# Seven products of quarters for the up product of three groups and the down product of all nine, a bank for the zeros, and a new order

## The chip, the cores and the metric

The kernel runs on one core of a Trainium2 chip. Its time is the time of one execution on the device, in microseconds (us). TensorE multiplies matrices into PSUM, an accumulator memory of eight banks of 2 KB a partition; VectorE (DVE) and ScalarE (ACT) read PSUM and the main on-chip memory, SBUF; GpSimd (POOL) works on SBUF. Each engine has its own queue of instructions and takes them strictly in the order written. An engine waits at an instruction until what it reads has been written and what it overwrites has been read.

## The reference

Eight sequences of 576 positions, eight heads of 64, float32. Causal attention within a window of 64 positions is followed by a feed-forward layer with a squared relu:

```
scores = q @ k.T / 8;  keep where 0 <= i - j < 64;  attn = softmax(scores)
x   = (attn @ v), heads side by side     # 4608 rows x 512
h   = max(x @ w_in, 0)                   # w_in 512 x 2048
out = (h * h) @ w_out                    # w_out 2048 x 512
```

## The kernel before

**Tiles and groups.** The 4608 rows are 36 tiles of 128 rows; four tiles make a group of 512 rows, two make a pair, and there are nine groups (the last four tiles hold the ends of all sequences). Matrices are held in SBUF in half precision (float16), products accumulate in float32.

**Order by hand.** The text `ORDER` (lines 16 to 93) is the program. Each word is a verb with numbers; the loop at the end calls the verb's function, which emits a few instructions on fixed engines. Since every engine works its queue in order, the order of the words is the order on every engine. A trailing number of many words picks the engine: 0 is POOL, 1 VectorE, 2 ScalarE.

**Attention.** `fk`, `fq`, `fv` load a tile of k, q, v from the SP queue; `kc`, `qc`, `vc`, `kp`, `qp` cast them to half precision, the later ones all on POOL; `vl`, `vh` copy v shifted by 64 rows. For the first eight tiles `T` transposes k and q on TensorE and `ck`, `cq` copy them out of PSUM; later tiles are transposed by a DMA (`tk`, `tq`). `S` makes scores (SS for a pair of tiles), `e` the exponential on ScalarE, `m` the mask on VectorE, `V` the product with v, `n` the division on VectorE, `X` with `x`, or `dx` by DMA, the transpose of the result, `xT`.

**Zeros.** `W`n (`warm`, line 331 on) multiplies n times by a tile of zeros. It writes into the unused part of the newest tile of attention's PSUM pool (`att_bank`), beside the transposed k and q, beside the product with v, or beside the transposed x. Each copy out of such a tile is after the zeros that were written into it.

**Up product.** Group 0 is made by pairs: `U` p.f makes two blocks of 128 columns of h for the 256 rows of pair p with eight products of 256 columns. The other groups use `P` g.f: one block of 128 for all 512 rows, four products of 512 columns. ScalarE's relu (`R`, `r`, line 468) takes the result out of PSUM, and `Q`, `s` square it, on ScalarE from the relu's copy (line 479) or on VectorE (line 481).

**Down product.** Group 0 uses `O`: four words for each of its four tiles of rows, four products of 512 columns each. Groups 1 to 8 use seven products of quarters instead of eight (the Strassen scheme in Winograd's form). `ws` forms sums of quarters of w_out once (line 492 on), `hs` g.i.half forms four sums of quarters of h for each group on VectorE (line 546, 1024 values a partition), `Z` g.n.half makes half of product n with eight products of 256 columns (line 557), and `ev` takes a finished bank out, on ScalarE or, where it is added to an earlier result, on VectorE (line 586). Product 2 reads sum 1, product 3 sum 0, product 4 sum 2 and product 5 sum 3; sum 1 reads sum 0, and sum 3 reads sum 1. `sd`, `sh`, `st` store rows of the output.

**PSUM.** Two banks belong to the up product (`ps_up`), two to the down product (`ps_out`; `U` takes from both in turn), and two tiles of two banks each to attention (`ps_att`).

**Weights.** `fw` 0 to 3 and `fo` 0 to 3 load quarters of w_in and w_out from POOL's queue, cast on the way.

## Time and profile before

| | |
|---|---|
| median of 3 runs | 297.95 us (297.55 to 298.44) |
| the profiled execution | 300.61 us, span 298.9 us |
| TensorE busy | 284.9 us (95% of the span) |
| VectorE, ScalarE, POOL busy | 198.4, 190.3, 106.2 us |
| granted TensorE clock, mean | 0.989 |
| moved by DMA | 55.52 MB, mean 186 GB/s |

The profile is of one execution. Its page gives each engine's busy time; the chain that ended last, followed back from the last instruction to whatever released each step; groups of like instructions; and waits, by the instruction that waited and what released it. Products on TensorE overlap each other, so the time that one shows (379 ns for 512 columns) is longer than the distance from one to the next; the distances are read from the chain in order of time. A line such as `DVE rden L416 <- PE av L337: 3.4, 2, 3.0` says that VectorE's instruction of line 416 stood 3.4 us in total, in two cases, at most 3.0, until TensorE's instruction of line 337 had ended.

### The profile page before, as it was taken

To read this page: it belongs to the slowest core of one execution; us is meant where nothing else is said; L and a number is where in the kernel's file an instruction comes from. 1 tells how busy PE (TensorE), PEld (TensorE's weight loads), DVE (VectorE), ACT (ScalarE), POOL (GpSimd) and SP (SyncE) were. 2 spreads that over 40 slices of the span, in tenths; PEclk is the share of its full clock that TensorE was granted. 3 is DMA by queue.
4 is the path that set the end of the run, shared out by engine and by line. 5 is a ranking of instruction groups with operands and counts; after the bars stand their busy time and mean duration, and the time that the engine had idled before them with its cause. 6 is when DMAs were issued, how large, how long until landed. Compare 5 with 4: busy or idle time off the path is not lost.

```text
span 298.9 us, 7277 instructions
## 1 busy us (share of the span) xinstructions
PE 284.9 (95%) x2922; PEld 187.7 (63%) x2922; DVE 198.4 (66%) x352; ACT 190.3 (64%) x307; POOL 106.2 (36%) x162
## 2 busy tenths in 40 slices
PE   7677989999999999999999999999999999999994
PEld 2445868444586656666765775675766666676783
DVE  3267864596694778749853995488658764756762
ACT  1647888676736978857589468948556847744400
POOL 2236821655674612761764087126131000000000
PEclk9699999999999999999999999999999999999999
DMA  6999999989999999999999999999999310300134
GB/s 189 262 217 293 217 197 196 229 175 239 255 215 224 199 200 252 228 191 226 214 211 237 195 256 237 209 218 227 246 212 194 108 37 0 143 0 2 70 107 105
DMA packets 162593, 55.52 MB, mean 186 GB/s; under 512 B 149248, under 2 KB 158464, under 8 KB 162560
## 3 DMA queue, kind: packets, MB, share of 16 engines
q1 hardware_dynamic: 157744, 50.35, 77.8%
q0 software_dynamic: 4224, 4.19, 8.6%
q10 hardware_dynamic: 592, 0.52, 0.6%
q8 instruction: 23, 0.38, 0.5%
q14 instruction: 10, 0.08, 0.1%
HBM read 38.80 MB, written 9.44 MB: 161 GB/s over the span
## 4 chain that ended last, share of the span: by engine, by line
PE 89%; ACT 4%; DVE 4%; DMA 1%; issue 0%; SPq 0%; DVEq 0%
PE hps L487 38%; PE opsC L557 10%; PE opsD L557 9%; PE opsA L557 9%; PE opsB L557 5%; PE ops L517 5%; PE av L410 4%; PE hps L457 3%; PE sc L385 3%; ACT kT L256 1%; DMA q_st<-in_q_dram 1%; DVE qT L258 1%; PE qkT_ps L337 1%; ACT pm L392 1%; PE xt_ps L427 1%; PE av L337 1%
## 5 line engine op out<-in xcount | busy, mean ns | idle before, releaser
L468 ACT ACTIVATE hrelu<-hps 128x512 f32<-128x512 f32 x144 | 85.0, 594 | 62.3 <-PE hps L487 57.0
L487 PE MATMUL hps<-xT,w_in_sb 128*128 128x512 f16 x512 | 123.4, 379 | 0.0
L487 PEld LDWEIGHTS <-w_in_sb 128*128 128x128 f16 x512 | 48.9, 98 | 46.1 <-issue 0.2
L557 PEld LDWEIGHTS <-h 128*128 128x128 f16 x640 | 61.9, 98 | 15.9 <-issue 0.3
L481 DVE SCALAR_TENSOR_TENSOR h<-hps,hrelu 128x512 f16<-128x512 f32 x57 | 39.1, 689 | 32.8 <-ACT hrelu L468 32.1
L479 ACT ACTIVATE h<-hrelu 128x512 f16<-128x512 f32 x87 | 54.5, 629 | 2.9 <-PE opsD L557 0.7
L392 ACT ACTIVATE pm<-sc 128x1024 f16<-128x1024 f32 x36 | 35.6, 1023 | 3.8 <-PE sc L385 3.8
L258 POOL CAST v_ev<-v_st 128x512 f16<-128x512 f32 x31 | 22.6, 728 | 41.5 <-DMA v_st<-in_v_dram 31.6
L258 POOL CAST k<-k_st 128x512 f16<-128x512 f32 x32 | 21.9, 685 | 35.3 <-DMA k_st<-in_k_dram 31.8
L557 PE MATMUL opsD<-wb_all,h 128*128 128x256 f16 x256 | 32.2, 273 | 0.0
L258 POOL COPY v_od<-v_ev 64x512 f16<-64x512 f16 x40 | 27.8, 697 | 8.0 <-DVE v_ev L258 5.7
L557 PE MATMUL opsA<-w_out_sb,h 128*128 128x256 f16 x240 | 30.3, 273 | 0.0
L557 PEld LDWEIGHTS <-hs_all 128*128 128x128 f16 x256 | 24.8, 98 | 6.6
L258 POOL CAST q<-q_st 128x512 f16<-128x512 f32 x28 | 19.4, 694 | 23.3 <-DMA q_st<-in_q_dram 17.6
L417 DVE TENSOR_TENSOR x_sb<-av,rden 128x512 f16<-128x512 f32 x36 | 24.9, 691 | 1.2
L397 DVE TENSOR_TENSOR pm<-pm,mask_inner 128x1024 f16<-128x1024 f16 x28 | 21.1, 758 | 6.3 <-ACT pm L392 6.1
L557 PE MATMUL opsB<-wb_all,hs_all 128*128 128x256 f16 x128 | 16.4, 273 | 0.0
L385 PE MATMUL sc<-qT,kT 64*128 64x64 f16 x512 | 12.1, 192 | 4.5 <-ACT kT L256 2.5
L557 PE MATMUL opsC<-w_out_sb,h 128*128 128x256 f16 x128 | 16.3, 273 | 0.0
L557 PE MATMUL opsC<-w_out_sb,hs_all 128*128 128x256 f16 x128 | 16.1, 273 | 0.0
L385 PEld LDWEIGHTS <-kT 64*128 64x128 f16 x512 | 9.8, 96 | 9.8 <-ACT kT L256 4.6
L517 PE MATMUL ops<-w_out_sb,h 128*128 128x512 f16 x64 | 15.6, 379 | 0.0
(80 smaller groups left out, 279.0 us busy)
## 6 DMA issues: line engine op xcount, KB each, us to landing
k_st<-in_k_dram SPq DMA_DIRECT2D x40, 256.0 KB, 4.5
v_st<-in_v_dram SPq DMA_DIRECT2D x40, 256.0 KB, 4.3
q_st<-in_q_dram SPq DMA_DIRECT2D x32, 256.0 KB, 4.4
out_dram<-osb_all SPq DMA_DIRECT2D x14, 512.0 KB, 3.6
w_in_sb<-in_moe_w_in_dram POOLq DMA_DIRECT2D x4, 512.0 KB, 8.5
w_out_sb<-in_moe_w_out_dram POOLq DMA_DIRECT2D x4, 512.0 KB, 15.9
out_dram<-osb_all SPq DMA_DIRECT2D x4, 256.0 KB, 2.8
q_st<-in_q_dram SPq DMA_DIRECT2D x8, 128.0 KB, 3.7
```

The source lines that it names most:

```text
L258: (nc.gpsimd, nc.vector)[e].tensor_copy(out=dst, in_=src)
L385: nc.tensor.matmul(scv[:, hh, hp, blk, :], keys[r0:r0 + 64, hp, k0:k0 + P], qT[r0:r0 + 64, hp, 64 * blk:64 * blk + 64], start=True, stop=True)
L392: nc.scalar.activation(out=pms[i][:, part], in_=scs[i][:, part], func=AF.Exp, scale=1.0 / float(D) ** 0.5)
L397: nc.vector.tensor_tensor(out=pms[i][:, part], in0=pms[i][:, part], in1=mask[:].rearrange("p (o a) b r -> p o (a b r)", o=1) .to_broadcast ...
L410: nc.tensor.matmul(avs[i][64 * blk:64 * blk + 64, h // 4, h % 4, 0:65], pms[i][:, h % 2, h0:h0 + 64], vv[:, h, 0:65], start=True, stop=True)
L417: nc.vector.tensor_tensor(out=x_of(i)[:, :, i % 2, :].rearrange("p (a b) (c d) -> p a b c d", a=2, c=2), in0=avs[i][:, :, :, 0:D].rearrang ...
L468: nc.scalar.activation(out=hr_of[key][:], in_=src, func=AF.Relu)
L479: nc.scalar.activation(out=dst, in_=hr, func=AF.Square)
L481: nc.vector.scalar_tensor_tensor(out=dst, in0=hps, scalar=0.0, in1=hr, op0=ALU.max, op1=ALU.mult)
L487: nc.tensor.matmul(hps[:], w_in_sb[:, c, f * P:(f + 1) * P], xT_of(g)[:, :, c, :], start=(c == 0), stop=(c == DMC - 1))
L517: nc.tensor.matmul(ops_of[ts][:], h2s[0][:, f, ts * P:(ts + 1) * P], w_out_sb[:, f, :], start=(f == 0), stop=(f == FFC - 1))
L557: nc.tensor.matmul(banks[bank][:, m, :], a[:, kk, m * P:(m + 1) * P], w[:, kk], start=(first and kk == 0 and m == 0), stop=(kk == KH - 1), ...
```

## The change

- `P` of group 1 becomes `U` of pairs 2 and 3, and the `O` words of group 0 become `Z`, `hs` and `ev`, as in the other groups.
- The up product of groups 6, 7 and 8 is made by seven products of quarters. `wq` n.u forms four sums of quarters of w_in for each of four units u (256 columns of each half), `xq` g.n four sums of quarters of xT, `Y` g.u.n product n of unit u with four products of 256 columns, `y` takes a bank out (ScalarE for n = 0, 1; VectorE adds an earlier result for the other five), and `yq` squares one of four finished quarters. A unit takes both banks of the up product and one attention tile (two banks).
- `hs`, `ws`, `wq`, `xq`, and the squares `Q`, `s` and `yq` (of product 1) can go to POOL with a last number of 0. In the new order these are 39 of 72 `hs` words, 3 `ws`, 9 `wq`, 10 `xq` and 17 squares.
- `W` takes its destination from the down product's banks: the first of them is kept for zeros until that pool's third tile, and afterwards the next tile that is due is taken in advance.
- In the last group, bank D of the down product becomes two half-filled banks, one for each half of the rows, evacuated apart.
- The identity is made in float32 and copied on POOL; a path for transposing float32 tiles is added and not used (`NF32 = 0`).
- Every word stands in a new order. Words change engine as well (`kc`, `qc`, `ck`, `cq`, `x`, `vc`, `vh`), and `fk0.1` and `fv1.1` load from ScalarE's queue. The zeros' products are 41 instead of 58, all 512 columns wide.

The order, in parts:

```diff
-A W9 ct cp fk0 cd fq0 fq1 fk1 cm fv0 kc0.1 fv1 fk2 qc0.1 fk3 T0 W3 qc1.0 fk4 ck0.1 cq0.2 kc1.2 fq2
-S0 vc0.1 e0 T1 W4 fq3 cq1.1 fq4 ck1.2 m0 fv2 S1 kc2.2 vc1.1 fv3 V0 W9 e1 n0 vh1.0 fv4 vl1.2 fk5 m1
...
-R1.4 fo2 V6 R1.5 V7 fo3 n6 U0.4 Q1.4.2 Q1.5.1 U1.7 R0.4 n7 U1.6 R1.7 kp8.0 fv10 Q0.4.1 Q1.7.2 X6
-X7 U0.7 R1.6 x7.1 x6.2 U0.6 R0.7 Q0.7.2 O0.0 R0.6 P1.15 Q1.6.2 Q0.6.1 P1.11 r1.15 s1.15.2 P1.3
-qp8.0 fk11 r1.11 O2.0 r1.3 s1.11.2 s1.3.1 P1.10 P1.7 r1.10 s1.10.1 O0.1 r1.7 s1.7.2 ws0.1 O0.2
...
+W10 ct cp fq0 cd fk0.1 fq1 fq2 fk1 cm fk2 fk3 qc0.1 fv0 fv1.1 kc0.2 fv2 T0 W3 qc1.0 fq3 cq0.1
+ck0.2 fk4 S0 W3 kc1.1 qc2.0 fq4 e0 T1 W1 fv3 kc2.2 m0 kc3.0 fv4 T2 W4 cq1.1 cq2.2 fk5 ck1.1 ck2.2
+vc0.1 S1 W1 fq5 vc1.1 e1 V0 W5 vh0.0 n0 fv5 vh1.0 vl1.2 fk6 h2 qc3.2 vc2.0 X0 x0.1 kc4.2 fq6 S2
+vh2.0 m1 T3 W2 e2 fv6 qc4.0 ck3.1 cq3.2 fw0 T4 fk7 vc3.1 S3 W2 ck4.1 cq4.2 vl2.0 fq7 e3 vl3.1
...
+vc4.0 V1 W2 fv7 n1 fw1 kc5.2 S4 W1 fk8 e4 m2 vh4.0 X1 W2 m3 qc5.0 x1.2 V2 n2 T5 W1 cq5.2 ck5.1 X2
+W1 x2.1 S5 m4 V3 W3 e5 vc5.0 fq8 n3 V4 fw2 vl5.2 X3 n4 U0.0 vh5.0 x3.1 X4 m5 kc6.0 fv8 R0.0 U0.1
...
+ck7.1 Q2.5.0 U0.7 vc7.1 R1.7 wq0.0.0 wq3.0 U1.4 R0.7 Q1.7.1 Q2.3.0 U2.2 Q0.7.1 wq0.1.0 R1.4 vl7.1
+S7 wq3.2 R2.2 wq1.2.0 U0.6 e7 wq1.0 fo3 U2.4 wq1.1 Q1.4.2 wq1.3.0 m7 fv10 R0.6 U2.7 R2.4 hs0.0.0
+Q0.6.0 V7 Q2.4.2 U2.6 n7 hs0.2.0.0 Q2.2.2 U1.6 wq2.2 R2.7 R2.6 kp8.0 Q2.7.1 X7 U2.1 Q2.6.2 wq2.1.0
+x7.1 hs0.1.0 R1.6 U3.0 ws0.0.0 R2.1 ws0.1 Q1.6.2 U3.5 ws3.1 fk11 R3.0 Q2.1.0 U3.3 hs0.0.1 Q3.0.2
...
+vc8.0 ws0.3 U3.6 fv11 Q3.7.2 vh8.0 ws3.3 R3.1 U3.4 fk12 kp9.0 hs0.1.1 R3.6 Z0.0.0 qp9.0 ws2.1 R3.4
+tk8 Q3.6.2 vc9.0 ws1.0 Z0.0.1 Q3.4.2 ws1.3 kp10.0 tq8 Z0.2.0 ev0.0 ws0.2 qp10.0 Q3.1.2 ws3.0
...
+fv22 P3.7 h18 r3.10 vh20.0 s3.10.1 Z2.2.1 hs2.3.1.0 r3.7 fk23 s3.7.1 P3.2 ev2.2 hs2.3.0.0 P3.12
+fq23 r3.2 ev2.3 SS9 s3.2.1 r3.12 dx16 kp20.0 Z2.5.0 e18 kp21.0 Z2.5.1 e19 qp21.0 tk20 m18 vc21.0
...
+qp24.0 sd2.1 r3.14 VV10 r3.9 s3.14.1 fk26 Z3.0.0 s3.9.2 n20 hs3.0.0.0 P3.13 n21 fq26 P4.2 r3.13
+hs3.1.0.0 h22 fv26 s3.13.2 Z3.0.1 r4.2 fk27 P4.1 ev3.0 hs3.2.0.0 s4.2.2 fq27 Z3.2.0 r4.1 kp25.0
...
+Z5.4.1 y7.1.0 y6.1.6 hs6.0.1.0 y7.3.0 yq6.1.5.1 SS16 yq6.1.6.2 ev5.3 Y7.1.1 hs6.1.1.0 tk35 ev5.4
+Y7.3.1 e32 Z5.5.0 hs6.0.0 tk34 e33 hs6.2.1.0 Z5.5.1 m32 y7.1.1 m33 Z5.6.0 y7.3.1 hs6.1.0.0 ev5.5
+Z5.6.1 sd5.0 xq7.0.0 VV16 ev5.6 yq7.3.1.2 Y7.2.0 xq7.2.0 yq7.1.1.2 n32 sd5.1 Z6.2.0 y7.2.0
+hs6.2.0.0 xq7.1 Z6.0.0 n33 Y7.2.2 xq7.3.0 dx32 Y7.2.1 y7.2.2 Z6.0.1 y7.2.1 yq7.2.1.0 SS17 ev6.0
+Y7.1.2 e35 Y7.3.2 y7.1.2 Z6.1.0 e34 y7.3.2 Z6.1.1 m35 m34 Y7.3.3 ev6.1 hs6.3.1.0 Y7.3.4 y7.3.3
...
+yq7.0.4.2 Z6.6.1 yq7.2.4.1 Y7.0.6 ev6.6 Y8.1.0 y7.0.6 Y7.0.5 sd6.1 y8.1.0 Y8.2.0 xq8.0 Y7.2.6
+yq7.0.6.1 y8.2.0 xq8.1.0 Y8.1.1 y7.2.6 Y8.2.1 y8.1.1 xq8.3.0 Z7.0.0 y7.0.5 yq7.2.6.2 yq8.1.1.0
+yq7.0.5.1 Y8.1.2 Y8.1.3 xq8.2.0 y7.2.5 y8.2.1 Z7.0.1 hs7.0.0.0 yq7.2.5.1 Y8.1.4 y8.1.2 ev7.0
+Y8.2.2 y8.1.3 Y8.2.4 hs7.0.1.0 Z7.1.0 y8.2.2 y8.1.4 Y8.2.3 yq8.2.1.0 Y8.1.5 yq8.1.4.2 y8.2.3
+Z7.1.1 hs7.1.0.0 y8.1.5 Y8.1.6 y8.2.4 ev7.1 Y8.0.0 hs7.2.0.0 yq8.1.5.2 y8.1.6 Z7.2.0 yq8.1.6.1
+Y8.2.6 y8.0.0 hs7.1.1.0 hs7.3.0 Y8.3.0 Y8.0.1 y8.2.6 y8.3.0 Z7.3.0 hs7.2.1.0 hs7.3.1 yq8.2.6.2
+Z7.2.1 yq8.2.4.1 Y8.3.1 y8.0.1 ev7.2 Z7.3.1 y8.3.1 yq8.0.1.0 yq8.3.1.2 Y8.0.2 ev7.3 Y8.2.5 y8.0.2
+Y8.3.2 Y8.3.3 y8.2.5 Z7.5.0 y8.3.2 yq8.2.5.2 Y8.0.3 y8.3.3 Z7.4.0 y8.0.3 Y8.3.4 Y8.0.4 y8.3.4
...
+yq8.0.6.1 Y8.3.5 Z7.6.0 y8.3.5 hs8.0.0.0 y8.3.6 Z8.1.0 yq8.3.5.2 yq8.3.6.1 Z7.6.1 hs8.2.0.0 ev7.5
+Z8.1.1 ev7.6 sd7.0 hs8.0.1.0 hs8.1.0 Z8.0.0 sd7.1 hs8.3.0 Z8.0.1 hs8.1.1 Z8.2.0 ev8.0 hs8.2.1
+hs8.3.1.0 Z8.2.1 ev8.1 Z8.3.0 sh8.0.0 ev8.2 Z8.3.1 Z8.4.0 ev8.3 Z8.4.1 Z8.5.0 ev8.4 Z8.5.1 sh8.1.1
```

The functions:

```diff
-        make_identity(nc, ident[:])
+        make_identity(nc, ident32[:])
+        nc.gpsimd.tensor_copy(out=ident[:], in_=ident32[:])
...
+    held, idle, taken = {}, {}, {"up": 0, "out": 0}
+
+    def psum_of(kind):
+
+        if kind in held:
+            return held.pop(kind)
+        if kind == "att":
+            return ps_att.tile([P, 2, 512], FP32, name="att", tag="ps_a")
+        if kind == "any":
+            turns.append(len(turns) % 2)
+            return psum_of(("up", "out")[turns[-1]])
+        pool, tag = (ps_up, "ps_u") if kind == "up" else (ps_out, "ps_o")
+        taken[kind] += 1
+        return pool.tile([P, 512], FP32, name=tag, tag=tag)
+
     def att_bank(name):
-        atts.append((ps_att.tile([P, 2, 512], FP32, name=name, tag="ps_a"), name))
-        return atts[-1][0]
-
-    atts, scs, avs, xps, tps = [], {}, {}, {}, {}
-
-    def warm(n):
-
-        t, name = next(e for e in atts[:-3:-1] if e[1] != "sc")
-        bank, c0 = (0, 4 * 66) if name == "av" else (1, 0)
+        return psum_of("att")
+
+    scs, avs, xps, tps = {}, {}, {}, {}
+
+    def warm(n, kind):
+
+
+        if not idle:
+            idle[0] = psum_of("out")
+        if taken["out"] < 3:
+            dst = idle[0][:]
+        else:
+            held[kind] = t = psum_of(kind)
+            dst = t[:, 0, :] if kind == "att" else t[:]
         for _ in range(n):
-            nc.tensor.matmul(t[:, bank, c0:512], zero[:, 0:P], zero[:, c0:512],
-                             start=True, stop=True)
-
-    def T(i):
-        ps = att_bank("qkT_ps")[:, 0, :].bitcast(FP16).rearrange(
-            "p (s t g hp) -> p s t g hp", s=2, hp=HP, t=4)
-        for s, nm in enumerate("kq"):
+            nc.tensor.matmul(dst, zero[:, 0:P], zero[:], start=True, stop=True)
+
...
+        elif e == 0:
+            nc.gpsimd.tensor_tensor(out=dst, in0=hr, in1=hr, op=ALU.mult)
...
+    wsums = {}
+
+    def w_in_sum(n, u, e=1):
+        lo, hi = slice(2 * P * u, 2 * P * u + 2 * P), slice(DFF // 2 + 2 * P * u, DFF // 2 + 2 * P * u + 2 * P)
+        b11, b12, b21, b22 = (w_in_sb[:, c, f] for c in (slice(0, 2), slice(2, 4)) for f in (lo, hi))
+        if 4 * u + n < 6:
+            wsums[n, u] = st16.tile([P, 2, 2 * P], FP16, name="wi", tag="c16", bufs=6)
+        else:
+            wsums[n, u] = wi_all[:, 4 * u + n - 6]
+        x, y, op = {0: lambda: (b22, b12, ALU.subtract), 1: lambda: (wsums[0, u], b11, ALU.add),
+                    2: lambda: (b21, wsums[1, u], ALU.subtract),
+                    3: lambda: (b12, b11, ALU.subtract)}[n]()
+        (nc.gpsimd, nc.vector)[e].tensor_tensor(out=wsums[n, u][:], in0=x[:], in1=y[:], op=op)
+
+    def up_seven(g):
+        xT = xT_of(g)
+        (a11, a12), (a21, a22) = [[xT[:, t, c] for c in (slice(0, 2), slice(2, 4))]
+                                  for t in range(2)]
+        S, banks, sums = {2: a21}, {}, {}
+
+        def xsum(n, e=1):
+            if n == 0:
+                S["t"] = attw.tile([P, 2, 2, 2 * P], FP16, name="xs", tag="kT", bufs=4)
+            if n == 3:
+                S["u"] = attw.tile([P, 2, 2, 2 * P], FP16, name="xs", tag="kT", bufs=4)
+            S[n] = (S["t"][:, 0], S["t"][:, 1], a21, S["u"][:, 0] if n == 3 else None)[n]
+            x, y, op = ((a21, a22, ALU.add), (S[0], a11, ALU.subtract),
+                        (a11, a21, ALU.subtract), (a12, S.get(1), ALU.subtract))[n]
+            (nc.gpsimd, nc.vector)[e].tensor_tensor(out=S[n], in0=x, in1=y, op=op)
+
+        def mult(u, n):
+            lo = slice(2 * P * u, 2 * P * u + 2 * P)
+            hi = slice(DFF // 2 + 2 * P * u, DFF // 2 + 2 * P * u + 2 * P)
+            if n == 0:
+                banks[u, "A"] = psum_of("up")[:]
+            elif n == 2:
+                banks[u, "B"] = psum_of("up")[:]
+            elif n in (3, 4) and (u, "C") not in banks:
+                t = psum_of("att")
+                banks[u, "C"], banks[u, "D"] = t[:, 0, :], t[:, 1, :]
+            x = (a11, a12, S.get(1), S.get(0), S.get(2), S.get(3), a22)[n]
+            w = (w_in_sb[:, 0:2, lo], w_in_sb[:, 2:4, lo], wsums.get((1, u)), wsums.get((3, u)),
+                 wsums.get((0, u)), w_in_sb[:, 2:4, hi], wsums.get((2, u)))[n]
+            out_ps = banks[u, "AABCDCD"[n]].rearrange("p (m t) -> p m t", m=2)
+            first = n in (0, 2, 3, 4)
+            for c in range(2):
+                for m in range(2):
+                    nc.tensor.matmul(
+                        out_ps[:, m, :], w[:, c, m * P:(m + 1) * P], x[:, c, :],
+                        start=(first and c == 0 and m == 0), stop=(c == 1),
+                        skip_group_check=True)
+
+        def evac(u, n):
+            src = banks[u, "AABCDCD"[n]]
+            if n == 0:
+                sums[u, 2] = stage.tile([P, 512], FP32, name="u2", tag="st")
+                nc.scalar.activation(out=sums[u, 2][:], in_=src, func=AF.Copy, scale=1.0)
+                return
+            if n in (2, 3):
+                to, add = (sums[u, 2], sums[u, 2])
+                if n == 3:
+                    to = sums[u, 4] = stage.tile([P, 512], FP32, name="u4", tag="st")
+            else:
+                to = hr_of["y", g, u, n] = hrp.tile([P, 512], FP32, name="hrelu", tag="hrelu")
+                if n == 1:
+                    nc.scalar.activation(out=to[:], in_=src, func=AF.Relu)
+                    return
+                add = sums[u, 4 if n == 4 else 2]
+            nc.vector.tensor_tensor(out=to[:], in0=src, in1=add[:], op=ALU.add)
+
+        def square7(u, n, e):
+            f0 = (0 if n in (1, 6) else KH) + 2 * u
+            t0 = 0 if n in (1, 5) else 2 * P
+            dst = h2_of(g)[:, f0:f0 + 2, t0:t0 + 2 * P]
+            hr = hr_of["y", g, u, n][:]
+            hrv = hr.rearrange("p (m t) -> p m t", m=2)
+            if n == 1 and e == 0:
+                nc.gpsimd.tensor_tensor(out=dst, in0=hrv, in1=hrv, op=ALU.mult)
+            elif e == 2:
+                if n > 1:
+                    nc.scalar.activation(out=hr, in_=hr, func=AF.Relu)
+                nc.scalar.activation(out=dst, in_=hrv, func=AF.Square)
+            else:
+                nc.vector.scalar_tensor_tensor(
+                    out=dst, in0=hrv, scalar=0.0, in1=hrv, op0=ALU.max, op1=ALU.mult)
+
+        return xsum, mult, evac, square7
+
+    ups = {}
+
+    def ups_of(g):
+        if g not in ups:
+            ups[g] = up_seven(g)
+        return ups[g]
+
+
...
-        def hsum(i, half):
+        def hsum(i, half, e=1):
             ks = slice(half * KH // 2, (half + 1) * KH // 2)
             x, y, op = ((A[1][0], A[1][1], ALU.add), (Sh[0], A[0][0], ALU.subtract),
                         (A[0][0], A[1][0], ALU.subtract), (A[0][1], Sh[1], ALU.subtract))[i]
-            nc.vector.tensor_tensor(out=Sh[i][:, ks], in0=x[:, ks], in1=y[:, ks], op=op)
+            (nc.gpsimd, nc.vector)[e].tensor_tensor(
+                out=Sh[i][:, ks], in0=x[:, ks], in1=y[:, ks], op=op)
+
+        def split(bank):
+
+            return g == NTB - 1 and bank == "D"
 
         def product(bank, a, w, half, first, by_rows):
             if first and half == 0:
-                pool, tag = (ps_up, "ps_u") if bank == "E" else (ps_out, "ps_o")
-                banks[bank] = pool.tile([P, 2, NH], FP32, name=f"ops{bank}", tag=tag)
+                t = psum_of("up" if bank == "E" else "out")[:].rearrange("p (m d) -> p m d", m=2)
+                banks[bank] = [t[:, m] for m in range(2)]
+                if split(bank):
+                    banks[bank][1] = psum_of("up")[:, 0:NH]
+                else:
+                    banks[bank].append(t)
             steps = [(kk, m) for kk in range(half * KH // 2, (half + 1) * KH // 2)
                      for m in range(2)]
             if by_rows:
                 steps = [(kk, half) for kk in range(KH)]
             for kk, m in steps:
                 nc.tensor.matmul(
-                    banks[bank][:, m, :], a[:, kk, m * P:(m + 1) * P], w[:, kk],
-                    start=(first and kk == 0 and m == 0), stop=(kk == KH - 1),
+                    banks[bank][m], a[:, kk, m * P:(m + 1) * P], w[:, kk],
+                    start=(first and kk == 0 and (m == 0 or split(bank))), stop=(kk == KH - 1),
                     skip_group_check=True)
```

213 lines of the change are left out of this document (114 added, 99 removed).

## The prediction

> **What bounds the kernel now.** I read the page's busy shares first, then the chain that ended last, then the stretches of 10 us, then the waits, and last single instructions in order of time. The page:
>
> ```profile
> PE 284.9 (95%) x2922; PEld 187.7 (63%) x2922; DVE 198.4 (66%) x352; ACT 190.3 (64%) x307; POOL 106.2 (36%) x162
> PE 89%; ACT 4%; DVE 4%; DMA 1%; issue 0%; SPq 0%; DVEq 0%
> ```
>
> TensorE is busy 95% of the span and is 89% of the chain. The stretches (us, then PE, PEld, DVE, ACT, POOL busy, granted clock, DMA share, GB/s) say where it is not:
>
> ```profile
> 10.00:20.00 10.00, 6.93 (x82) 4.09 (x81) 4.93 (x11) 4.72 (x8) 4.68 (x7) 0.71 1.08 243
> 20.00:30.00 10.00, 7.93 (x136) 5.59 (x134) 7.42 (x15) 7.34 (x11) 4.78 (x7) 1.00 1.10 276
> 230.00:240.00 10.00, 10.00 (x97) 6.61 (x95) 7.33 (x11) 7.93 (x14) 0.00 (x0) 1.00 0.48 145
> 280.00:290.00 10.00, 10.00 (x90) 8.59 (x88) 7.66 (x12) 1.71 (x3) 0.00 (x0) 1.00 0.24 79
> ```
>
> From 50 to 290 us TensorE has no gap, so there a product taken out shortens the run by its own length. POOL is empty after 230 us. The chain in order of time (start, us, what) has the lengths of the products, and in the start the products of zeros:
>
> ```profile
> 9.66 1.72 PE qkT_ps L337 x4
> 11.40 0.70 DVE qT L258
> 13.97 1.99 PE av L337 x9
> 15.98 0.22 DVE rden L416
> ...
> 245.75 1.73 PE hps L487 x8
> 247.48 0.87 PE opsC L557 x8
> ```
>
> Eight up products of 512 columns are 1.73 us, so a P word (four) is 0.863. Eight products of 256 columns are 0.873 (0.87 here), the length of a Z or a U word; an O word is four of 512 columns again, 0.863, and a Y word of four of 256 is 0.437. In the start VectorE copies a transposed tile only after the zeros that were written beside it in the same tile; the waits show it:
>
> ```profile
> DVE rden L416 <- PE av L337: 3.4, 2, 3.0
> DVE qT L258 <- PE qkT_ps L337: 3.0, 2, 2.5
> DVE xT L258 <- PE xt_ps L337: 1.7, 3, 1.1
> DVE kT L258 <- PE qkT_ps L337: 1.1, 1, 1.1
> ```
>
> **TensorE's work.** P words fall from 128 to 64 (-64 x 0.863 = -55.2 us), the 16 O words go (-13.8), U words rise from 16 to 32 (+16 x 0.873 = +14.0), Z from 112 to 126 (+14 x 0.873 = +12.2), and 84 Y words come (+84 x 0.437 = +36.7). Sum **-6.1 us**, of which the seven products in the last three groups are 41.4 - 36.7 = 4.7. Attention's products are the same. All of it lies on the path as long as nobody else becomes late.
>
> **The start.** Between 0 and the first O word (51.05 us) TensorE does 25.5 us of needed work, by the lengths above, and loses 25.6. Nine pieces of zeros lie on the chain there: 0.66 + 1.72 + 1.99 + 0.45 + 0.23 + 0.45 + 0.60 + 0.23 + 0.59 = 6.9 us. With a bank of their own no copy waits for them; they still hold TensorE's queue for their own length. Bounds: 0 gained (the loads, whose share is 1.08 to 1.21 of the DMA engines between 10 and 50 us, are late next) to 6.9. I take **-4.5**, nearer to the upper end, because waits for loads are 7% of the chain up to 52 us and come at its beginning; and group 1 by pairs gives TensorE 16 more words to do before tile 7 has landed. If the zeros hold the clock less well, the second half-speed stretch (clock 0.71) is there in both.
>
> Small edits of the start. k0 and v1 are issued from ScalarE's queue. k0 now stands behind the table load and the first exponential, which end at 2.30; in the trace its 0.81 to 4.12 us from issue to use is 3.3, so it would be usable at 5.6, against 5.35 for q0, the later of the two so far: +0.3 us, inside the bounds above. SP's queue gets the next loads two issues earlier. The extra copy of the identity is some 0.3 us on POOL (its select of that tile is 0.29), needed at 4.65 us with POOL idle until 6.83. On POOL's queue the last w_out quarter now stands behind five squares and six sums, at a place where TensorE has 28 us of work done, thus at about 49 us; w_in's quarters land 8.5 us after issue, w_out's 15.9. Its first reader (the sum 0 of rows 6) stands at 37.5 us of work, about 59. So it costs 0 by the first row and 6 by the second, where VectorE's queue would stand. I take 0: the quarters are no longer issued four together. Group 0's four stores become two of 512 KB; SP's store queue has no reader on the chip.
>
> **The sums on POOL.** 39 of the 72 sums of h (1024 halves a partition) and 39 operations of 512 elements (sums of weights and of x, squares) go to POOL, which had none with two inputs. No row prices them. From below: one input, 0.61 us for 512 (POOL's casts when alone), so 0.6 and 1.2. From above: each operand as a pass of its own, 1.2 and 2.4. Nearest: on VectorE a second operand raises 512 halves from 0.30 (copy v_od, 0.301) to 0.43 (the shortest L504, 0.424), a factor of 1.42; POOL's 0.61 becomes 0.87, and 1024 about 1.6. I take **0.87 and 1.6**. What that costs is read from the order, as TensorE's work between the first of a run of POOL's sums and the product that reads the last:
>
> - group 7: five of 512 and three of 1024 (from xq8.1 to Z7.2.0) against 11 Y and 4 Z, 8.3 us: 4.35 + 4.8 = 9.15, short by 0.9. Then two more of 1024 before Z7.2.1, against 3.1: 0.1.
> - group 6: four of 1024 (hs6.0.1 to Z6.2.0) against 6.2: 0.2.
> - group 2: two (hs2.3.1, hs2.3.0, then Z2.5.0) against 2.4: 0.8.
> - group 3: two against 3.5: 0. Group 8: three and one VectorE sum of 0.69 before Z8.2.1 against 5.2: 0.3.
>
> Together 2.3; I take **+2**, since some of the 512s may be shorter. At 1.2 it is 0, at 2.0 some 9, at 2.4 some 16.
>
> **The last three groups on the other engines.** From the first Y word on TensorE has 88.4 us of work. VectorE has 60 additions of products, 22 evacuations of the down product, 15 squares, 10 sums, 4 masks, all at 0.69 (L586, L481, L546 alone), and 6 normalisations at 0.89, two x sums at 0.45: 82.8 us. Back to back it starts one each 0.61, which makes 73 to 74. In the kernel before the same three groups were 94.7 us of TensorE's and 64 of VectorE's. So VectorE goes from two thirds to 83 to 94%, in order, while each unit of Y holds both of up's banks until VectorE has read them: bounds 0 and 6 (next part). I take **+2.5**. ScalarE: 24 evacuations at 0.59, 29 squares of which most need a relu of their own first (0.60 + 0.63), about 55 us with attention's four exponentials: it stays below.
>
> **The end.** After the last product VectorE reads both halves of bank D, 0.76 us, since they are one bank; with a bank for each half only the second is left, 0.42: **-0.3**.
>
> **Sum.** The profiled execution took 300.6 us (span 298.9). 300.6 - 6.1 - 4.5 + 2 + 2.5 - 0.3 = 294.2. The median of the runs shown is 2.66 below the profiled execution, so **291.5 us**. Own range 285 (6.9 in the start, no cost elsewhere) to 296.
>
> **Rivals.**
>
> *POOL sums of 2.4 us make TensorE wait (slower).* Place: the products Z.2, Z.5 and Z.3 named above. The shortfalls become 4.9 + 1.7 + 3.4 + 2.4 + 1.3 + 2.7 = 16.4 instead of 2: 306 us. It decides from just under 2.0 us on (some 8.5 us, no gain left). For it: a half-precision copy of 64 x 512 and a cast from single precision both take POOL 0.61, so POOL gains nothing from halves, while VectorE's 0.69 for 1024 halves lives on that. Against: that bound lets POOL read each operand in a pass of its own, and VectorE pays only 1.42 for the second. The Trainium skill, GPSIMD Engine Reference, section 3.1, holds just that: two-input operations run at some 2.6 cycles an element since both reads share a port, 4497 ns for 2048; by it a sum of 1024 would be an estimated 2.25 us and this kernel take about 303. No row here shows a POOL operation with two inputs. Chance 0.34.
>
> *VectorE bounds the last three groups.* VectorE and POOL block each other, as these show:
>
> ```profile
> 117.60 1.10 DVE L546 TENSOR_TENSOR h<-h,hs_all 128x1024 f16<-128x1024 f16 x1
> ...
> 117.53 0.63 POOL L258 CAST v_ev<-v_st 128x512 f16<-128x512 f32 x1 [9.10 <-PE opsA L557]
> 118.22 0.95 POOL L258 COPY v_od<-v_ev 64x512 f16<-64x512 f16 x1
> ```
>
> The sum waited 0.41 for the cast, and the copy then 0.34 for the sum. If each of the 29 VectorE operations with both inputs in SBUF (squares, sums, masks) pays 0.41, VectorE needs 82.8 + 11.9 = 94.7 against 88.4: 6.3 lost instead of 2.5, and one or two more where a bank comes free late: 297. Against: in the kernel before POOL's blocking never reached TensorE, and 0.61 per start leaves room. Chance 0.12.
>
> *The zeros' bank gains nothing, as loads are late next*: 296. For it: waits of POOL's casts for v loads, 12.9 us before 52. Chance 0.10.
>
> **How the numbers follow.** The forecast has 0.44. Changes under 0.3% can't be told from none. Faster: nearly all of 0.44, 0.03 of the first rival, 0.07 of the second, 0.08 of the third, 0.61 or so; same 0.01 + 0.02 + 0.03 + 0.01 = 0.07; slower 0.32, nearly all POOL's. The range starts at the forecast's lower end, 285, and goes to 307, just above POOL's upper bound, whose case can't be left out.
>
> **What will show it.** Right: no wait of qT, kT, rden or xT for L337; the first Z word of group 0 by 62 us (39.5 of work and some 21 lost); TensorE without gaps from 45 us to the end; POOL sums of 1024 at or under 1.7. Wrong: PE waiting for POOL hs_all or h, with sums above 2; VectorE at 9.5 of 10 in the stretches after 200 us with PE under 9.5; a start that ends as late as before.

## The result, and the profile after

The changed kernel takes **342.99 us** (median of 4 runs, 338.33 to 345.98), the kernel before 298.11 on the same chip: a ratio of 1.142 (95% interval 1.130 to 1.155). Ratios and intervals here leave out runs more than 1.5% above the fastest of their kernel, so they can differ a little from the ratio of the medians. The forecast was 291.5, its range 285 to 307. The profiled execution has a span of 340.8 us and a mean granted clock of 0.950, against 298.9 and 0.989.

The page's busy shares and its chain, of the changed kernel:

```profile
PE 295.5 (87%) x3161; PEld 216.1 (63%) x3161; DVE 253.6 (74%) x377; ACT 185.6 (54%) x300; POOL 242.1 (71%) x242
DVE 6%; PE 6%; POOL 6%; issue 6%; ACT 0%; POOLq 0%; ACTq 0%; DVEq 0%
```

TensorE was 95% busy and 89% of the chain. The chain of the changed kernel can be followed back only as far as 251 us, which is why its shares are so small; on that piece no engine carries it. POOL went from 106 to 242 us, VectorE from 198 to 254. The stretches of 10 us (PE, PEld, DVE, ACT, POOL busy, granted clock, DMA share, GB/s):

```profile
50.00:60.00 10.00, 6.67 (x53) 5.22 (x54) 8.76 (x11) 4.82 (x10) 7.51 (x8) 0.66 1.18 243
80.00:90.00 10.00, 5.68 (x67) 4.22 (x65) 9.93 (x11) 1.42 (x3) 9.83 (x8) 0.80 0.46 110
250.00:260.00 10.00, 5.73 (x76) 4.67 (x75) 9.88 (x10) 4.68 (x8) 9.84 (x6) 1.00 0.01 2
```

Where TensorE is at 5.7 of 10, POOL and VectorE are both full, and with few instructions: in 250 to 260 us POOL does 6 and VectorE 10. The groups say why. First POOL's (a sum of 1024, a square of 512), then VectorE's (mask, addition of a product of up, two kinds of square):

```profile
L682 POOL TENSOR_TENSOR h<-h 128x1024 f16<-128x1024 f16 x13 | 30.6, 2360 | 1.9 <-DVE hs_all L682 1.6
L519 POOL TENSOR_TENSOR h<-hrelu 128x512 f16<-128x512 f32 x13 | 13.7, 1060 | 8.9 <-ACT hrelu L506 8.8
```

```profile
L440 DVE TENSOR_TENSOR pm<-pm,mask_inner 128x1024 f16<-128x1024 f16 x28 | 29.7, 1074 | 11.0 <-ACT pm L435 10.7
L615 DVE TENSOR_TENSOR hrelu<-att,u 128x512 f32<-128x512 f32 x36 | 23.7, 684 | 6.2 <-PE att L594 3.7 <-POOL h L624 2.1
L521 DVE SCALAR_TENSOR_TENSOR h<-ps_u,hrelu 128x512 f16<-128x512 f32 x30 | 20.4, 685 | 16.9 <-ACT hrelu L506 16.8
L630 DVE SCALAR_TENSOR_TENSOR h<-hrelu 128x512 f16<-128x512 f32 x15 | 17.4, 1163 | 0.3
```

A sum of 1024 takes POOL 2.25 to 2.39 us by group, not the 1.6 that I took, and an operation of 512 takes 1.06 to 1.6, not 0.87. VectorE's operations that read one operand from a PSUM bank (att, ps_u) keep their 0.68; those with both inputs in SBUF are longer: the square 1.16, and the mask 1.07, which was 0.76 in the kernel before:

```profile
L397 DVE TENSOR_TENSOR pm<-pm,mask_inner 128x1024 f16<-128x1024 f16 x28 | 21.1, 758 | 6.3 <-ACT pm L392 6.1
```

Lines in order of time show one such meeting (start, us, what):

```profile
48.12 1.33 POOL L559 TENSOR_TENSOR wi_all<-wi_all,w_in_sb 128x512 f16<-128x512 f16 x1
48.36 4.31 DVE L559 TENSOR_TENSOR wi<-wi,w_in_sb 128x512 f16<-128x512 f16 x2
49.40 0.81 POOL L221 DMA_DIRECT2D w_out_sb<-in_moe_w_out_dram  x1
50.23 1.16 POOL L559 TENSOR_TENSOR wi_all<-wi_all,w_in_sb 128x512 f16<-128x512 f16 x1
51.34 1.04 POOL L519 TENSOR_TENSOR h<-hrelu 128x512 f16<-128x512 f32 x1
52.60 0.68 DVE L440 TENSOR_TENSOR pm<-pm,mask_inner 128x1024 f16<-128x1024 f16 x1
53.33 0.51 PEld L453 LDWEIGHTS <-pm 128*64 128x64 f16 x16 [4.91 <-DVE pm L440]
```

Two VectorE sums of 512, 0.42 each in the run pool_writes_only below, take 4.31 us (1.37 and 3.02) beside three operations of POOL and its issue of a load. The mask behind them waits, TensorE's product of values behind the mask waits 4.9 us, and its clock is then granted at half speed (0.66 in that stretch). Where sums of POOL follow each other the two engines take turns, and both are longer: the masks 2.60, the sums 2.56.

```profile
82.04 2.56 POOL L682 TENSOR_TENSOR hs_all<-hs_all,h 128x1024 f16<-128x1024 f16 x1
82.54 2.60 DVE L440 TENSOR_TENSOR pm<-pm,mask_first 128x1024 f16<-128x1024 f16 x1
84.55 2.56 POOL L682 TENSOR_TENSOR h<-h,hs_all 128x1024 f16<-128x1024 f16 x1
85.06 2.60 DVE L440 TENSOR_TENSOR pm<-pm,mask_inner 128x1024 f16<-128x1024 f16 x1
```

The waits of TensorE, for masks and for sums:

```profile
PEld L453 <- DVE pm L440: 17.8, 10, 4.9
PEld L702 <- POOL hs_all L682: 4.0, 3, 2.4
PEld L702 <- DVE hs_all L682: 4.0, 4, 2.4
```

TensorE waits longest for VectorE's masks. Its direct wait for POOL's sums is short; what these delay through VectorE is not in that row. The clock lost 340.8 x (1 - 0.950) = 17 us of TensorE's full speed, before 298.9 x 0.011 = 3.

**A measure for all runs.** The table has the experiments that follow below. For each pair of tiles I take the start of its first product of scores and subtract TensorE's work that the order has before it, by the lengths of the prediction (0.875 for a Z or U word; attention's by their rows: scores 0.33, values 0.36, transposes 0.50 and 0.25 a tile). The rest is what TensorE has lost so far, in us; "end" is the span less all of its work (the old order 268.1, the changed one 262.0, the two with pairs 268.3). Each row is one execution: code_old_order and old_order_pool_678, whose starts are the same, have 26.0 and 25.0 at tiles 8 and 9, so a difference of 1 us says little.

| kernel | tiles 8, 9 | 10, 11 | 18, 19 | 22, 23 | 30, 31 | 34, 35 | end |
|---|---|---|---|---|---|---|---|
| before | 25.5 | 25.6 | 25.9 | 26.0 | 26.1 | 26.2 | 30.8 |
| changed | 29.5 | 36.6 | 43.9 | 44.8 | 47.1 | 59.5 | 78.8 |
| sums_on_vector | 26.7 | 29.5 | 34.3 | 34.6 | 35.4 | 45.0 | 57.4 |
| pool_writes_only | 28.7 | 29.0 | 34.8 | 37.8 | 39.0 | 42.0 | 54.5 |
| pool_half_sums | 24.0 | 27.5 | 28.8 | 30.3 | 34.3 | 40.3 | 49.3 |
| pool_short_writes | 20.0 | 20.0 | 25.7 | 27.8 | 32.0 | 35.6 | 43.2 |
| short_writes_fewer_loads | 20.0 | 20.0 | 20.3 | 20.4 | 20.5 | 22.6 | 30.8 |
| changed_fewer_loads | 28.8 | 35.1 | 39.6 | 42.0 | 45.1 | 57.2 | 76.3 |
| code_old_order | 26.0 | 26.0 | 26.6 | 26.6 | 26.8 | 26.8 | 31.0 |
| pairs_then_old_order | 22.9 | 24.0 | 24.5 | 24.5 | 24.6 | 25.8 | 30.0 |
| pairs_later_attention | 22.7 | 23.9 | 24.3 | 26.1 | 29.1 | 30.8 | 35.6 |

### The profile page after: what moved, and what is told of

Read it like the earlier page. It is cut to its first block, busy times and chain, and to the rows that moved or that the text cites. A ratio compares the mean times of both kernels' runs of the same rounds, so it can differ in the third digit from the quotient of the medians.

```text
span 340.8 us, 7893 instructions
## 1 busy us (share of the span) xinstructions
PE 295.5 (87%) x3161; PEld 216.1 (63%) x3161; DVE 253.6 (74%) x377; ACT 185.6 (54%) x300; POOL 242.1 (71%) x242
## 5 line engine op out<-in xcount | busy, mean ns | idle before, releaser
L506 ACT ACTIVATE hrelu<-ps_u 128x512 f32<-128x512 f32 x80 | 47.2, 594 | 38.2 <-PE ps_u L527 30.7
L527 PE MATMUL ps_u<-xT,w_in_sb 128*128 128x512 f16 x256 | 63.4, 387 | 2.0 <-DVE h L521 1.7
L702 PE MATMUL ps_o<-w_out_sb,h 128*128 128x256 f16 x416 | 52.4, 276 | 1.8 <-DVE u L736 1.4
L435 ACT ACTIVATE pm<-att 128x1024 f16<-128x1024 f32 x36 | 35.7, 1022 | 17.6 <-PE att L428 17.5
L702 PEld LDWEIGHTS <-hs_all 128*128 128x128 f16 x288 | 29.1, 105 | 16.2 <-POOL hs_all L682 4.0
L702 PE MATMUL ps_o<-wb_all,h 128*128 128x256 f16 x272 | 37.2, 281 | 0.0
L521 DVE SCALAR_TENSOR_TENSOR h<-ps_u,hrelu 128x512 f16<-128x512 f32 x30 | 20.4, 685 | 16.9 <-ACT hrelu L506 16.8
L517 ACT ACTIVATE h<-hrelu 128x512 f16<-128x512 f32 x51 | 31.9, 630 | 1.2
L682 POOL TENSOR_TENSOR h<-h 128x1024 f16<-128x1024 f16 x13 | 30.6, 2360 | 1.9 <-DVE hs_all L682 1.6
L495 PEld LDWEIGHTS <-w_in_sb 128*128 128x128 f16 x256 | 25.5, 102 | 7.0 <-issue 1.9
L615 DVE TENSOR_TENSOR hrelu<-att,u 128x512 f32<-128x512 f32 x36 | 23.7, 684 | 6.2 <-PE att L594 3.7
L460 DVE TENSOR_TENSOR x_sb<-att,rden 128x512 f16<-128x512 f32 x36 | 24.9, 691 | 1.2
L682 POOL TENSOR_TENSOR h<-h,hs_all 128x1024 f16<-128x1024 f16 x10 | 22.4, 2249 | 4.1 <-PE ps_o L702 2.5
```

Source lines behind the costliest of these rows:

```text
L435: nc.scalar.activation(out=pms[i][:, part], in_=scs[i][:, part], func=AF.Exp, scale=1.0 / float(D) ** 0.5)
L460: nc.vector.tensor_tensor(out=x_of(i)[:, :, i % 2, :].rearrange("p (a b) (c d) -> p a b c d", a=2, c=2), in0=avs[i][:, :, :, 0:D].rearrang ...
L495: nc.tensor.matmul(hps[:, f, :], w_in_sb[:, c, (2 * f2 + f) * P:(2 * f2 + f + 1) * P], xT_of(p // 2)[:, p % 2, c, :], start=(c == 0), stop ...
L506: nc.scalar.activation(out=hr_of[key][:], in_=src, func=AF.Relu)
L517: nc.scalar.activation(out=dst, in_=hr, func=AF.Square)
L527: nc.tensor.matmul(hps, w_in_sb[:, c, f * P:(f + 1) * P], xT_of(g)[:, :, c, :], start=(c == 0), stop=(c == DMC - 1))
```

## The experiments

My theory after the result: POOL's sums are too long for the places that the order gives them, and while POOL reads two operands VectorE can't, so that VectorE's masks and sums come late too. The rivals: the order itself, with its seven products of up, binds; or the start's gain isn't there.

**sums_on_vector.** All 78 two-input operations of POOL on VectorE, in their places.

```diff
-hs6.0.1.0 hs6.1.1.0 xq7.0.0 yq7.2.1.0 Q0.4.0
+hs6.0.1 hs6.1.1 xq7.0 yq7.2.1.1 Q0.4.1
```

> The changed kernel with its order kept, but all 78 two-input operations of POOL (sums of h, of the weights and of x, squares) on VectorE instead. Theory A (POOL's two-input operations are the cause, 2.3 us where the order leaves 1.5, and while they read SBUF they hold up VectorE's own two-input operations): VectorE's waits inside its instructions go (masks 1.07 and 1.28 us back to 0.69, sums 1.1 to 1.5 back to 0.69), TensorE waits only where VectorE has too much, in the last three groups (102 us of VectorE's at 0.69 each against 88 of TensorE's): 300 to 312 us. Theory B (the seven up products and the order itself are the cause, POOL only looks busy): no less than 330.

Measured 320.14 us, ratio 1.072 (1.065 to 1.078), between the ranges of the two theories. The 23 us come off at once, masks are back at 0.80 to 0.86. But VectorE is now overfull, in 50 to 80 us with group 0's sums and again in the last three groups:

```profile
60.00:70.00 10.00, 8.09 (x73) 6.87 (x72) 9.96 (x17) 6.17 (x11) 7.07 (x10) 1.00 1.01 220
280.00:290.00 10.00, 7.85 (x58) 6.24 (x58) 9.97 (x18) 5.53 (x10) 0.00 (x0) 0.83 0.00 0
```

So the sums have no place on VectorE either; the run doesn't say what POOL's length and the blocking are worth apart.

**pool_writes_only.** POOL keeps about its time and its places, but almost only writes.

```diff
-tt(out=..., in0=..., in1=..., op=op)          # POOL, each of 78
+nc.gpsimd.memset(out, 0.0)
+nc.gpsimd.memset(out, 0.0)
+nc.gpsimd.tensor_tensor(out=col(out), in0=col(in0), in1=col(in1), op=op)   # two columns
```

> The changed kernel with each of POOL's 78 two-input operations replaced by two fills of the same output (they read nothing) and a sum of two columns; it leaves out those sums and squares, so its output is not the reference's. The fills should take about 1.9 us for 1024 values and 1.0 for 512, by the constants' fills (0.20 for 128 columns, 0.15 for 64), near the 2.3 and 1.15 of the sums. Theory A1 (the blocking: VectorE's two-input operations wait while POOL reads): masks back to 0.69 us, time at or under 315. Theory A2 (the length: results from POOL come late for TensorE, blocking is a detail): masks at 0.69 too, but the time stays at 328 or more.

Measured 319.49 us, 1.070 (1.063 to 1.077), again between the two theories. A fill of 1024 takes 0.95, so a pair of fills and its small sum some 2.2. With POOL as long as that, VectorE's mask is at 0.79 and its busy time at 208.8 us in place of 253.6:

```profile
L492 POOL MEMSET hs_all<- 128x1024 f16 x16 | 15.2, 953 | 0.9
L440 DVE TENSOR_TENSOR pm<-pm,mask_inner 128x1024 f16<-128x1024 f16 x28 | 21.9, 794 | 11.8 <-ACT pm L435 11.5
```

POOL's reading costs some 23 us of the 45. (A fill needs no operand, so it can start before the sum in its place could have; the 23 hold that too.) By the table, the changed kernel loses 8 us more than this run as far as tiles 30 and 31, and 16 more after them. The Trainium skill's SBUF — State Buffer, "Who interferes with whom", has this rule: a VectorE instruction with two SBUF inputs contends with a GpSimd instruction that reads SBUF and not with one that only writes, and one with at most one SBUF input does not contend, outside VectorE's two-port modes. The rows agree on the first two points, with 1.07 for the mask beside sums and 0.79 beside fills; for the third they have 0.68 for the operations whose other operand is in PSUM. VectorE's cast of v, with one input, is longer too: 0.64 in the changed kernel, 0.44 in sums_on_vector.

**code_old_order and old_order_pool_678.** The changed kernel's functions with the old order: the zeros' bank and the split of bank D alone; then the 24 sums of groups 6 to 8 on POOL besides.

```diff
-ORDER of the changed kernel
+ORDER of the kernel before, without its first word
# the second:
-hs6.0.0 hs7.0.1 hs8.1.0
+hs6.0.0.0 hs7.0.1.0 hs8.1.0.0
```

> The functions of the changed kernel with the order of the kernel before (only its first word, which took a tile for the zeros, is left out): the zeros' bank and the split of the last bank alone. By the forecast's terms -4.5 and -0.3: 293 us, no wait of qT, kT, rden and xT for the zeros. Rival (loads are late next, or the zeros still hold TensorE's own queue): 296 to 298.

> The same as code_old_order, but the 24 sums of h in groups 6, 7 and 8 on POOL, which has nothing else to do after 230 us. The price by itself: 1024 halves in 2.3 us or a little less with nothing beside it. Theory A2 (length): each half of a group has a chain of two sums before product 2 or 3; the order leaves some 0.7 to 2 us for each, so each half loses 1 to 3 us: code_old_order plus 6 to 16 us. Theory A1 (blocking only): VectorE has few two-input operations there, so under 4 us more.

The first: 300.70 us, 1.006 (1.002 to 1.010), which is 2.3 above the 298.37 of the kernel before in that series and longer than either expectation. No copy waits for zeros any more, but nothing is gained; the chain of its first 20 us consists of issues of loads and of one load of v:

```profile
10.64 9.53 DMA v_st<-in_v_dram
```

The second: 312.89, 1.048 (1.041 to 1.054), 12.2 us more than the first, 0.5 for each of 24 sums: here the length costs. POOL has nothing else to do there, so these rows are its own price of a sum, 2.12 to 2.20 us:

```profile
L669 POOL TENSOR_TENSOR h<-h 128x1024 f16<-128x1024 f16 x6 | 13.1, 2180 | 0.1
L669 POOL TENSOR_TENSOR hs_all<-h 128x1024 f16<-128x1024 f16 x6 | 12.7, 2124 | 23.8 <-DVE h L508 14.7 <-ACT h L504 8.8 <-PE att L415 0.3
```

**pool_short_writes and pool_half_sums.** What if POOL had had about the prediction's lengths (1.6 and 0.87)? One fill in place of two (1.3 us for 1024, 0.77 for 512, little reading); or half the sum and a fill of the other half (1.22 + 0.52 = 1.74 and 0.65 + 0.3 = 0.95, half of the reading).

```diff
-nc.gpsimd.memset(out, 0.0)
-nc.gpsimd.memset(out, 0.0)
+nc.gpsimd.memset(out, 0.0)          # pool_short_writes; two-column sum stays
# pool_half_sums: memset of the second half, tensor_tensor of the first half
```

> The changed kernel in its own order, but each of POOL's 78 operations with two inputs becomes one fill of its output and a sum of two columns: some 0.95 + 0.24 = 1.2 us in place of 2.1 for 1024 elements, 0.53 + 0.24 = 0.77 in place of 1.05 for 512 (the lengths that the run with two fills showed for its parts), and next to nothing that VectorE has to wait for. The sums and squares of POOL are left out. Theory: POOL's length and the blocking are the whole cause, so everything else that was forecast holds: 288 to 296 us (forecast 291.5, and 1.2 is below the 1.6 that it counted), no wait of TensorE for POOL's hs_all, masks at 0.70 to 0.80. Rival: the order itself binds (banks of the up products that VectorE must empty first, or the start): over 303 us, with TensorE waiting for VectorE or ScalarE after 200 us.

> The changed kernel in its own order, but each of POOL's 78 operations with two inputs does only the first half of its columns and fills the other half: about 1.1 + 0.53 = 1.6 us for 1024 elements and 0.56 + 0.29 = 0.85 for 512, which are the lengths that the prediction counted (1.6 and 0.87), with the blocking of VectorE for about half of what the changed kernel has. Half of each of POOL's sums and squares is left out. Theory: length is what failed, and the blocking costs in proportion to the time that POOL reads two inputs: 300 to 312 us (the run with the short fills, plus some half of the 23 us that the blocking cost at full length). Rival A: at the forecast's lengths the blocking is absorbed by VectorE's slack, as the prediction counted: 291 to 297. Rival B: VectorE's waits are a matter of chance order and remain nearly whole: over 320.

Measured 306.10 (1.019, 1.012 to 1.027; four runs between 302.70 and 309.55) and 312.72 (1.045, 1.039 to 1.050). My theory of that moment fell: even with POOL shorter than I had counted, the kernel is slower than before. The table shows where: at tiles 8 and 9 TensorE has lost 20.0 us, 5.5 less than before, and then gives the lead back, 7.8 by tiles 22 and 23. The chain of the short run from 180 us on, its transfers:

```profile
180.73 5.04 DMA k_st<-in_k_dram
...
187.23 3.38 DMA v_st<-in_v_dram
...
192.57 4.29 DMA v_st<-in_v_dram
...
201.53 3.95 DMA k_st<-in_k_dram
...
209.09 4.67 DMA k_st<-in_k_dram
```

Tiles 18 and 19 begin at 122 us, and tiles 30 and 31 at 199, in this run and in the kernel before alike. That pointed to the loads.

**short_writes_fewer_loads and changed_fewer_loads.** 23 of the 108 loads of q, k and v out, in the short run and in the changed kernel.

```diff
+if nm == "v" and 8 < i: return                       # fetch
-sts["v", i][:]
+sts["v", min(i, 8)][:]                               # cast_v; tile 8 in a buffer of its own
-tile_pool(name="stage", bufs=14)
+tile_pool(name="stage", bufs=13)
```

> The run pool_short_writes with 23 of the 108 loads of q, k and v taken out: tiles 9 to 31 take their v from a tile that is loaded once (so v of these tiles is left out, as are POOL's sums and squares), and the staging ring has 13 buffers in place of 14. In pool_short_writes TensorE had lost 20.0 us when it reached the scores of tiles 8 and 9, 5.5 less than in the kernel before (25.5), but 27.9 at tiles 22 and 23 (before 26.0) and 35.6 at tiles 32 and 33 (before 26.2), with the DMA engines' share at 0.9 to 1.2 throughout and k, q and v loads on the chain. Theory: the loads set the pace of attention, the lead of the start is given back to them: with a fifth fewer the lost time stays within 20 to 24 us as far as tiles 22 and 23, and the run ends at 291 to 298 us. Rival: the waits come from the order of the engines' work and not from the loads: lost time again 27 or more at tiles 22 and 23, and 303 to 307 us.

> The changed kernel, all of POOL's sums and squares in it, with the same 23 loads of v taken out and 13 staging buffers (v of tiles 9 to 31 is left out). Theory: with POOL's sums at 2.1 to 2.4 us TensorE comes so late (29.5 us lost at tiles 8 and 9, 43.9 at tiles 18 and 19) that the loads are no longer what it waits for; the loads bound only what remains when POOL is relieved: 336 to 345 us, no change against the changed kernel's 343. Rival: the loads cost the changed kernel their 11 us as well, whatever POOL does: 328 to 334 us.

The first: **294.68 us**, 0.986 (0.978 to 0.993), and the lost time stays at 20.0 to 20.5 as far as tiles 30 and 31. The same stretch with all loads, then without the 23:

```profile
90.00:100.00 10.00, 7.48 (x100) 4.49 (x100) 4.25 (x8) 6.06 (x10) 5.72 (x12) 1.00 1.02 235
```

```profile
90.00:100.00 10.00, 10.00 (x116) 5.87 (x115) 5.47 (x9) 9.27 (x15) 7.45 (x15) 1.00 1.15 204
```

The second: 343.42, no change against 342.99. The loads are a bound behind POOL's: they cost 11.4 us only where POOL is out of the way. Which part of a load binds is not told apart: its transfer, SP's queue, in which loads, transposes and stores stand in order, or the ring of staging buffers. Leaving the loads out relieves all three.

**pairs_then_old_order and pairs_later_attention.** Is the start's lead worth anything without the rest? The new order's words up to the first Z (without sums of w_in and w_out and group 0's), then the old order from its first O word, without group 1's P words. In the second, attention's words come up to 4.5 us later from tiles 18 and 19 on.

```diff
-A W9 ct cp fk0 ... Q1.6.2 Q0.6.1 P1.11 ... O0.0 O2.0 ...      (old)
+W10 ct cp fq0 ... U3.4 R3.6 R3.4 Q3.6.2 ... O0.0 O2.0 ...     (new start, old rest)
```

> The new order's first 330 words (tiles 0 to 7, groups 0 and 1 up by pairs of tiles, 32 U words, zeros in their bank; no sums on POOL, squares of POOL on VectorE), then the old order's words from the first O word on, without group 1's P words; O for group 0, P for groups 2 to 8. TensorE has as much work as before. Theory: the start's lead of 5.5 us is real and is kept as long as loads allow: they had 5 to 8 us of slack at the scores of tiles 10 to 23 in the kernel before and 0.4 to 2.3 from tiles 28 on, so some 1 to 3 us of the lead are left at the end: 296 to 298 us. Rival: nothing is left of it, and more is lost where queues are out of step with each other: 299 to 303.

> As pairs_then_old_order, but from tiles 18 and 19 on the words of attention (scores, exponentials, masks, values, normalisation, transposes of x) come later among the words of the network, by up to 4.5 us of TensorE's work, so that TensorE asks for q and k at about the clock times of the kernel before although it is ahead by the start's lead. Theory: the loads are what takes the lead back, and work that needs no loads can fill in: 293 to 296 us, faster than before. Rival: later attention makes group 8's x late instead, or the lead was never there: 298 to 303 us.

The first: **296.58 us** (10 runs), 0.994 (0.990 to 0.997), the one version of the whole computation that is faster than the kernel before, by 1.6 us of 298.15. Of the lead 2.6 us are left at tiles 8 and 9 and 1.5 at tiles 30 and 31 (its profiled execution took 300.04, longer than the median, so these are low). The second: 305.22, 1.021 (1.014 to 1.028): TensorE loses 4.8 us between tiles 18 and 30, where the first run loses 0.1. Later attention did not use the lead; which queue lost the time I haven't followed up.

**vector_sums_old_up and old_order_up_seven_last.** The seven products of up by themselves: taken out of the changed kernel with all sums on VectorE; and put into the old order for group 8 alone (this order takes the sum hs8.2.1 before a product that should have read its operand as it was, so a part of group 8's output is another; the work is the same).

```diff
-Y6.0.0 y6.0.0 ... yq6.0.4.1 ...        (groups 6 to 8)
+P6.0 r6.0 s6.0.2 ...
# the second, in the old order:
-P8.11 r8.11 s8.11.2 ...
+Y8.0.0 Y8.0.2 y8.0.0 y8.0.2 Y8.0.3 Y8.0.4 ... yq8.0.5.1 yq8.0.6.1
```

> The changed kernel in its own order with all sums and squares of POOL on VectorE, and in groups 6 to 8 the up product again by eight products of 512 columns (P) with their relu and square, in the places of the Y words. The start, group 0's seven products of the down product and the zeros' bank stay. TensorE has 6.1 - 4.7 = 1.4 us less to do than before. Theory: what is left of the loss in the run with all sums on VectorE (320.1) is VectorE's load in the last three groups, 84 evacuations of up banks, and 16 sums of w_in: 296 to 303 us, VectorE below 9 of 10 after 210 us. Rival: group 0's sums and the 80 first us are the cause: 310 or more, with VectorE at 9.8 or more of 10 between 50 and 80 us and TensorE's work there late by over 8 us, as in that run.

> The kernel before in its old order with the bank of zeros, and only group 8's up product by seven products of quarters: 28 Y words in the places of its 16 P words, their evacuations and squares on VectorE and ScalarE right behind, the 16 sums of w_in on VectorE between groups 6 and 7, none of the sums on POOL. TensorE has 16 x 0.863 - 28 x 0.437 = 1.6 us less to do. Theory: the seven products themselves are worth their length where nobody else is late: 298.5 to 300 us, against 300.7 for the old order without them. Rival: the units hold up's banks until VectorE and ScalarE have emptied and squared them: waits of TensorE for y's evacuations of 3 us or more, 303 to 308 us.

The first: 319.11, 1.056 (1.050 to 1.062), which is the rival's time but not its place: only 25.0 us were lost at tiles 10 and 11, the rest came after 100 us, partly where VectorE is at 4 to 6 of 10. A likely reason, not tested, is that my words of P stand where Y words stood. The run tells nothing on the seven products, and I leave it. The second: 309.36, 1.032 (1.026 to 1.037), some 8 more than code_old_order; TensorE waits for the banks until VectorE has added up the unit's products:

```profile
PE att L584 <- DVE hrelu L605: 5.1, 5, 1.4
```

That is the rival's mechanism, in an order of mine with squares and additions right behind each unit, for one group. The changed kernel's own order, with two units in turn, has 2.2 us of that wait for three groups where POOL is short (pool_short_writes).

## Why the prediction was wrong

The spans of four runs of the changed order make an account, read as steps of one path (in another order of the steps the shares would differ, as changed_fewer_loads shows): 292.8 with short fills and fewer loads, 305.2 with all loads, 316.5 with POOL at 2.2 us without reading, 340.8 with reading. So: loads 12.4, POOL's length from 1.3 to 2.2 some 11.3, the blocking of VectorE 24.3. These are single executions, and those of pool_short_writes alone lie 6.9 apart, so a share can be off by some 3 us.

1. *TensorE's work, -6.1*: right. In the chain of pool_short_writes eight products of 512 columns take 1.73 us, eight of 256 take 0.87 and four 0.44, as counted. (That work, start and last groups make up the span without the other costs, 298.9 - 6.1 - 5.5 + 5.6 = 292.9 against 292.8 measured, only repeats how the table is made. In medians that run is 3.5 us below the kernel before, 294.68 against 298.15.)
2. *The start, -4.5*: the lead is there (5.5 by tiles 8 and 9 where POOL is short, within the bounds of 0 and 6.9), but its cause and its place were not as forecast, and its size owes something to luck. The profiled execution of the kernel before has TensorE at half clock from about 9 to 16 us (0.71 granted in 10 to 20) and takes 2.5 us more than the median; 28 of 34 other executions of it have a mean clock of 0.996 or more. Two of the nine pieces of zeros lie in that half clock: 1.72 for four products of 512 columns, which are 0.86 at the pace of a P word, and 1.99. So some 1.9 of the 6.9 were half clock, which the step of -2.66 to the median took off once more, and against a usual execution the lead is an estimated 3 (5.5 - 2.5, if all of that lies in the start) to 5.5. Nor is that stretch "there in both": the changed kernel is granted 1.00 up to 50 us. The zeros' bank gains nothing by itself (code_old_order, 26.0 lost against 25.5): there the third rival is right, loads are late next. The lead comes from the new order of the start (pairs_then_old_order, with that order alone, has 22.9). And with all loads in, it isn't kept: attention runs at the pace of the loads, whose share is about 1 of the DMA engines from 10 to 220 us, and TensorE waits for them until it is as late as before. I had looked at the loads only up to 52 us, and read "no gaps after 50" as TensorE being the only bound; by these runs the kernel before was near two bounds at once. The first Z word came at 59 us where POOL is short (forecast: by 62), and at 67 in the changed kernel.
3. *POOL's sums, +2*: **this step failed**, in its price and in the path that it looked at. 1.6 us had been scaled from VectorE's ratio of two inputs to one; the rows say 2.12 to 2.20 alone and 2.25 to 2.39 here. The Trainium skill's GPSIMD Engine Reference, section 3.1, by which I had estimated 2.25, agrees with these rows. The first rival, with 2.4 and 306 us, failed as well: it counted only products that wait for a POOL sum, at the places of the list, in groups 2, 3 and 6 to 8. Its 16.4 at 2.4 looks like the 11.3 measured from 1.3 to 2.2, but by luck: 8.7 of these are lost before tiles 8 and 9 (28.7 against 20.0), among the sums of the weights and of group 0, which the list doesn't have. One wait of TensorE in pool_writes_only makes half of it:

```profile
PE ps_o L719 <- POOL wb_all L493: 4.6, 1, 4.6
```

   And the step left out that two-input work on POOL stops two-input work on VectorE, the largest share.
4. *VectorE in the last three groups, +2.5*: the second rival had the blocking, with a price of 0.41 an operation, but for 29 operations of the last groups and with the casts of POOL in mind. It is paid wherever POOL sums, and most there: 16 of the 24 us come after tiles 30 and 31. VectorE's busy time grows by 44.8 us between pool_writes_only and the changed kernel, on the masks of attention, the sums of h and the squares, and TensorE then waits for the masks and has its clock halved (17 us against 3). Without POOL's reading and with loads out of the way the last groups cost 10.3 us from tiles 30 and 31 to the end against 4.7 before: +5.6, near the upper of my bounds 0 and 6, and more than the 4.7 that the seven products take off TensorE's work there.
5. *The end, -0.3*: right. From the end of the last product to that of VectorE's last read it is 0.80 before and 0.45 with the split bank.
6. *Small edits*: no run tells them apart. Of those that the prediction lists code_old_order has only the identity's copy; the others belong to the new order.

The sign "no wait of qT, kT, xT, rden for L337" came out as forecast, and code_old_order shows how little it says: the waits went and the time stayed.

## What to carry to other kernels

Before work is moved to an idle engine, price it by that engine's own rows for the same number of inputs, and ask which other engine shares its way to memory: the bill came largely on VectorE's masks, which the change did not touch. A TensorE without gaps can hide a second bound that lies just behind it; to see it, compare when each transfer lands with when it is first used, over the whole span. And an order fits the durations that it was made for: of six that I made from the two orders by a simple rule, one was faster than the kernel before, by 0.6%.
